# Attention tiled by 128 instead of 112 queries, the last 64 queries of two heads over one another, V loaded by batch

## The chip, the cores and the metric

The kernel runs on one core of a Trainium2 chip. A core has a matrix engine (PE, which loads weights and then streams columns through them), a vector engine (DVE), a scalar engine (ACT), a general engine (POOL), and a queue engine (SP) that issues most loads. Times are device microseconds of the whole program. The time of a kernel is the median of its runs.

## The reference

Causal attention over 4 batches, 12 heads, 448 positions and 64 dimensions a head, all in f32. The heads are then joined into rows of 768, which go through an MLP with a leaky activation.

```python
scores = scale * np.matmul(q, k.transpose(0, 1, 3, 2))   # q, k, v: (4, 12, 448, 64)
scores = np.where(mask, -1000000000.0, scores)           # mask: keys after the query
scores = scores - np.max(scores, axis=-1, keepdims=True)
attn = np.exp(scores)
attn = attn / (np.sum(attn, axis=-1, keepdims=True) + 1e-09)
attn_out = np.matmul(attn, v)
x = attn_out.transpose(0, 2, 1, 3).reshape(4 * 448, 768)
h = x @ w_in                                             # (768, 2048)
g = np.maximum(h, 0.0) + alpha * np.minimum(h, 0.0)
out = g @ w_out                                          # (2048, 768)
```

## The kernel before

The work has two parts. The first is attention, over 24 pairs of heads (`pairs`: four batches of six). The second is the MLP, whose weights arrive as 64-bit floats and are taken apart on the chip into two f32r pieces each (`decode_piece`, on DVE, POOL and ACT); its matmuls (`h_unit`, `o_tile`) begin while the last pairs of attention are still under way.

In attention the head's dimension lies on the partitions: a pair has head 0 on partitions 0 to 63 and head 1 on 64 to 127 (`half(j)`). The 448 queries are cut into four chunks of `CP` = 112. For each pair p, chunk i and head j:

- `load` (steps LQ, LK) brings Q and K, and `load_v` (LV) brings V of this pair: 112 rows of 2 KB.
- `scores` (S0, S1, S2) multiplies query chunk i with the keys up to its end. The two heads' matmuls use different rows of the array and run side by side; each head has its own PSUM bank. S0 makes chunks 1 and 0, S1 chunk 2, S2 chunk 3.
- `row_max` (MXij, DVE) adds the mask, scales, and takes the row's minimum in one pass, in place.
- `row_exp` (EXij, ACT) takes the exponential and the row's sum; `row_rec` (RC, DVE) the reciprocals of all eight sums of the pair; `row_norm` (NOij, POOL) multiplies.
- `transpose_p` (PTi, PE) transposes the probabilities in blocks of 112 by 112, 20 of them a pair; `pt_copy` (Cij, ACT or DVE) copies them out of PSUM into `ptf`, block c of chunk i at place i + 3c.
- `av` (AV) multiplies them with V, for each block c of keys all queries from there on. The two heads use different columns of the array and write the two halves of one bank.
- `x_hi` and `x_lo` (XH, XL) split the result into two f32r pieces for the MLP.

The order of all this is written out by hand in `ORDER`, which `attention` walks once per step n: an entry `NAME+lag` runs the step for pair n - lag, and a letter a, d or p says ACT, DVE or POOL. So in one step PE does AV of pair n - 4, transposes of n - 3 and scores of n - 1. Each engine works through its instructions strictly in this order and waits on semaphores. `early_steps`, `h_next` and `decode_start` are hung on entries of the last pairs. ED is one instruction of the decoding of the first weights, in each step from pair 4 on.

PSUM has eight banks, given out by `bank` in the order of their release. A pair takes 13 of them: six for scores, six for transposes, one for AV.

Of the kernel before, what the change touches and what calls it, by code (L numbers as in the profile page):

```python
# [32 lines left out]
def kernel(  # L33
# [132 lines left out]
    def load_v(p):
        b, hp = pairs[p]
        T["v", p] = ap["v"].tile([CP, NCH, 2, D], F32, tag="v", name=f"v_{p}")
        nc.sync.dma_start(out=T["v", p].rearrange("p c j d -> p (c j) d"), in_=v[b, hp])

    def copy(out, x, eng, side=1.0):
        if eng is nc.scalar:
# [4 lines left out]
            eng.tensor_scalar(out=out, in0=x, scalar1=side, scalar2=1.0, op0=ALU.mult, op1=ALU.mult)  # L177


    def scores(p, n):  # L180


        banks = [bank(f"s_{p}_{n}_{j}")[:CP] for j in range(2)]
        o = 0
        for i in ((1, 0), (2,), (3,))[n]:
            lim = (i + 1) * CP
            for j, ps in enumerate(banks):
                nc.tensor.matmul(  # L188
                    ps[:, o : o + lim], T["q", p][half(j), i * CP : (i + 1) * CP],
                    T["k", p][half(j), :lim], start=(o == 0), stop=(n > 0 or i == 0),  # L190
                )
            for j, ps in enumerate(banks):
                T["s", p, i, j] = ps[:, o : o + lim]
            o += lim

    def row_max(p, i, j):


        t = T["s", p, i, j]
        nm = T["nm", p, i, j] = ap["b4"].tile([CP, 1], F32, tag="nm", name=f"nm_{p}_{i}_{j}")  # L200
        nc.vector.tensor_tensor_reduce(  # L201
            out=t, in0=t, in1=maskb[:, (NCH - 1 - i) * CP :], scale=-SCALE, scalar=MOST_F32,
            op0=ALU.add, op1=ALU.min, accum_out=nm,
        )

    def row_exp(p, i, j):
        lim = (i + 1) * CP
        if ("p", p, i) not in T:
            T["p", p, i] = ap["p"].tile([CP, 2, lim], F32, tag=f"p{i}", name=f"p_{p}_{i}")
        if ("sm", p) not in T:  # L210
            T["sm", p] = ap["b2"].tile([CP, 2 * NCH], F32, tag="sm", name=f"sm_{p}")
        z = 2 * i + j
        nc.scalar.activation(  # L213
            T["p", p, i][:, j], T.pop(("s", p, i, j)), AF.Exp, scale=-1.0,
            bias=T.pop(("nm", p, i, j)), accum_out=T["sm", p][:, z : z + 1],
        )
# [12 lines left out]
    def transpose_p(p, i, *heads):
        t = T["p", p, i]
        for js in heads:
            ps = bank(f"pt_{p}_{i}_{js[0]}")[:CP, : len(js) * (i + 1) * CP]
            ps = T["pt", p, i, js] = ps.rearrange("p (j c n) -> p j c n", j=len(js), n=CP)
            for j in js:
                for c in range(i + 1):
                    nc.tensor.transpose(  # L238
                        ps[:, j - js[0], c], t[:, j, c * CP : (c + 1) * CP], ident[:CP, :CP]
                    )  # L240

    def pt_copy(p, i, js, eng):
        if ("ptf", p) not in T:
            T["ptf", p] = ap["pt"].tile([CP, 2, 3 * NCH + 1, CP], F32, tag="ptf", name=f"ptf_{p}")
        copy(T["ptf", p][:, js[0] : js[-1] + 1, i : 4 * i + 1 : 3], T.pop(("pt", p, i, js)), eng)

    def av(p):

        out = T["a", p] = bank(f"a_{p}")[:, :S]
        for c in range(NCH):  # L250
            for j in range(2):
                x = T["ptf", p][:, j].rearrange("p x n -> p (x n)")
                nc.tensor.matmul(  # L253
                    out[half(j), c * CP :], T["v", p][:, c, j],
                    x[:, 4 * c * CP : (3 * c + NCH) * CP], start=(c == 0), stop=(c == NCH - 1),
                )

    def x_cut(p):
# [7 lines left out]
        h, l = x_cut(p)  # L266
        nc.vector.tensor_tensor(out=l, in0=T.pop(("a", p)), in1=h, op=ALU.subtract)
# [12 lines left out]
    for i in range(NCH):  # L280
        heads = ((0, 1),) if i < 2 else ((0,), (1,))
        add(steps, f"PT{i}", transpose_p, i, *heads)
        for js in heads:
            add(choice, f"C{i}{js[0]}", pt_copy, i, js)
        for j in range(2):
# [245 lines left out]
```

## Time and profile before

| | |
|---|---|
| median of three runs | 651.55 us (650.79 to 652.76) |
| the profiled execution | 650.67 us, span 648.9 us |
| granted PE clock, mean | 0.995 |
| attention, first scores to the end of pair 23's scores | 5.1 to 164.3 us |
| overlap of attention's end with the MLP | 164.4 to 231.8 us |
| MLP alone | 231.8 to 648.9 us |

The busy share of an engine counts every moment in which one of its instructions runs. For PE that is any part of its array. "PEld" is PE's weight loading, which overlaps its matmuls. In a timeline a row begins with its start and length in us, joins equal instructions that follow each other (x16), and ends with the idle time before it and what ended that, where there was any. A group's row ends with its count, busy time and the mean of one in ns.

### The profile page before, as it was taken

The page shows a single profiled execution, that of the slowest core. Times are in us where ns is not written, and L with a number is a line of the kernel's source. Part 1 is how long each engine was busy: PE and PEld are TensorE (multiplying, and loading weights), DVE is VectorE, ACT ScalarE, POOL GpSimd, SP SyncE. Part 2 cuts the span into 40 slices and gives each one's busy share as a digit, 9 for nine tenths or more (in the row PEclk, how much of TensorE's full clock was granted, in tenths as well). Part 3 has the DMA queues.
Part 4 walks back from the last instruction along what each step waited for, and adds up shares of the span by engine and source line. Part 5 has one row for each costly group of instructions (what it writes and reads, how often), then busy time and mean ns, then how long its engine had stood idle before and what let it go on. Part 6 is the DMA issues. An engine that isn't in the chain of part 4 may idle for free.

```text
span 648.9 us, 10886 instructions
## 1 busy us (share of the span) xinstructions
PE 639.7 (99%) x3753; PEld 547.4 (84%) x3753; DVE 473.8 (73%) x1213; ACT 227.0 (35%) x662; POOL 296.6 (46%) x394
## 2 busy tenths in 40 slices
PE   7999999999999999999999999999999999999997
PEld 4667767667679989998999999899989999998997
DVE  4688787787785866887877777677877678775444
ACT  6789988889523432111111111111111111111010
POOL 3456566565555534454433434454344435443110
PEclk8999999999999999999999999999999999999999
DMA  5434434336050302032002203020330202000223
GB/s 141 135 88 111 145 98 113 99 94 200 5 195 0 97 2 97 1 98 80 19 22 78 97 1 99 27 71 1 97 98 1 78 21 98 0 2 2 97 98 146
DMA packets 32439, 47.90 MB, mean 74 GB/s; under 512 B 5248, under 2 KB 23936, under 8 KB 32384
## 3 DMA queue, kind: packets, MB, share of 16 engines
q1 hardware_dynamic: 32224, 46.98, 23.2%
q8 instruction: 30, 0.49, 0.3%
q10 hardware_dynamic: 160, 0.23, 0.1%
q14 instruction: 25, 0.20, 0.1%
HBM read 41.69 MB, written 5.51 MB: 73 GB/s over the span
## 4 chain that ended last, share of the span: by engine, by line
PE 87%; POOL 5%; issue 4%; DVE 3%; ACT 1%; POOLq 0%; DVEq 0%; ACTq 0%
PE o L352 33%; PE h L318 31%; PE a L253 8%; PE pt L238 7%; PE s L188 7%; POOL p L177 2%; ACT p L213 1%; POOL gl L338 1%; PE warm L147 1%; POOL wi L128 1%; POOL wo L128 1%; POOL y_i L124 1%; POOL y_o L124 0%; DVE g L328 0%; DVE x_i L115 0%
## 5 line engine op out<-in xcount | busy, mean ns | idle before, releaser
L352 PE MATMUL o<-wo,gh 128*128 128x384 f32 x896 | 229.3, 337 | 0.9 <-DVE g L332 0.9
L318 PE MATMUL h<-xh,wi 128*128 128x512 f32 (+1 forms) x768 | 218.2, 364 | 0.1
L338 POOL TENSOR_TENSOR gl<-g,gh 128x512 fp32r<-128x512 f32 (+1 forms) x64 | 74.2, 1159 | 254.8 <-ACT gh L337 237.6
L352 PEld LDWEIGHTS o<-wo,gh 128*128 128x128 f32 x896 | 162.3, 188 | 3.2 <-DVE g L332 1.2
L318 PEld LDWEIGHTS h<-xh,wi 128*128 128x128 f32 x768 | 138.6, 189 | 22.7 <-ACT ptf L173 0.3
L352 PE MATMUL o<-wo,gl 128*128 128x384 f32 x448 | 150.7, 336 | 0.0
L337 ACT ACTIVATE gh<-g 128x512 fp32r<-128x512 f32 (+1 forms) x64 | 37.0, 579 | 297.6 <-DVE g L332 297.6
L318 PE MATMUL h<-xl,wi 128*128 128x512 f32 (+1 forms) x384 | 139.4, 363 | 0.0
L360 DVE TENSOR_TENSOR acc<-o,acc 128x384 f32<-128x384 f32 x196 | 102.9, 553 | 42.7 <-PE o L352 41.5
L177 POOL TENSOR_SCALAR p<-p,rs 112x224 f32<-112x224 f32 (+1 forms) x192 | 92.9, 505 | 73.1 <-PE s L188 46.1
L213 ACT ACTIVATE p<-s,nm 112x224 f32<-112x224 f32 (+1 forms) x192 | 93.8, 496 | 25.9 <-DVE nm L201 25.3
L328 DVE TENSOR_SCALAR g<-h,alpha_sb 128x512 f32<-128x512 f32 (+1 forms) x64 | 43.5, 680 | 75.5 <-POOL gl L338 48.2
L201 DVE CUSTOM_DVE_ANT_0 s<-s,maskb 112x224 f32<-112x224 f32 (+1 forms) x192 | 79.9, 478 | 7.1 <-PE s L188 7.1
L352 PEld LDWEIGHTS o<-wo,gl 128*128 128x128 f32 x448 | 84.1, 188 | 0.0
L318 PEld LDWEIGHTS h<-xl,wi 128*128 128x128 f32 x384 | 72.4, 189 | 10.4
L253 PEld LDWEIGHTS a<-ptf,v 112*64 112x64 f32 x384 | 36.4, 136 | 39.2 <-issue 13.8
L253 PE MATMUL a<-ptf,v 112*64 112x448 f32 (+3 forms) x384 | 65.3, 406 | 0.1
L238 PE MATMUL pt<-ident,p 112*112 112x112 f32 x480 | 53.5, 267 | 3.6 <-POOL p L177 2.7
L238 PEld LDWEIGHTS pt<-ident,p 112*112 112x112 f32 x480 | 47.5, 136 | 8.4 <-POOL p L177 3.9
L188 PE MATMUL s<-kr,qr 64*112 64x224 f32 (+3 forms) x384 | 54.3, 414 | 0.0
L173 ACT ACTIVATE ptf<-pt 112x224 f32<-112x224 f32 (+1 forms) x96 | 41.0, 488 | 4.0 <-PE pt L238 4.0
L332 DVE SCALAR_TENSOR_TENSOR g<-h,g 128x512 f32<-128x512 f32 (+1 forms) x64 | 40.0, 625 | 2.2
(42 smaller groups left out, 528.3 us busy)
## 6 DMA issues: line engine op xcount, KB each, us to landing
wi<-in_moe_w_in_dram SPq DMA_DIRECT2D x32, 384.0 KB, 4.4
wo<-in_moe_w_out_dram SPq DMA_DIRECT2D x32, 384.0 KB, 5.5
qr<-in_q_dram SPq DMA_DIRECT2D x48, 112.0 KB, 2.7
v<-in_v_dram SPq DMA_DIRECT2D x24, 224.0 KB, 3.0
kr<-in_k_dram SPq DMA_DIRECT2D x46, 112.0 KB, 2.8
out_dram<-acc SPq DMA_DIRECT2D x13, 384.0 KB, 2.3
out_dram<-acc SPq DMA_DIRECT2D x2, 192.0 KB, 1.9
kr<-in_k_dram ACTq DMA_DIRECT2D x2, 112.0 KB, 3.6
```

Source lines behind the costliest of these rows:

```text
L173: eng.activation(out, x, AF.Copy, scale=side)
L177: eng.tensor_scalar(out=out, in0=x, scalar1=side, scalar2=1.0, op0=ALU.mult, op1=ALU.mult)
L188: nc.tensor.matmul(ps[:, o : o + lim], T["q", p][half(j), i * CP : (i + 1) * CP], T["k", p][half(j), :lim], start=(o == 0), stop=(n > 0 or ...
L201: nc.vector.tensor_tensor_reduce(out=t, in0=t, in1=maskb[:, (NCH - 1 - i) * CP :], scale=-SCALE, scalar=MOST_F32, op0=ALU.add, op1=ALU.min ...
L213: nc.scalar.activation(T["p", p, i][:, j], T.pop(("s", p, i, j)), AF.Exp, scale=-1.0, bias=T.pop(("nm", p, i, j)), accum_out=T["sm", p][:, ...
L238: nc.tensor.transpose(ps[:, j - js[0], c], t[:, j, c * CP : (c + 1) * CP], ident[:CP, :CP])
L253: nc.tensor.matmul(out[half(j), c * CP :], T["v", p][:, c, j], x[:, 4 * c * CP : (3 * c + NCH) * CP], start=(c == 0), stop=(c == NCH - 1),)
L318: nc.tensor.matmul(ps[:, :T], w[kk], x[:, kk, t0 : t0 + T], start=(n == 0), stop=(n == 3 * KD - 1),)
L328: nc.vector.tensor_scalar(out=t[:, :T], in0=ps, scalar1=0.0, scalar2=alpha_sb[:, ch : ch + 1], op0=ALU.min, op1=ALU.mult,)
L338: nc.gpsimd.tensor_tensor(out=gl[:, :T], in0=t[:, :T], in1=gh[:, :T], op=ALU.subtract)
L352: nc.tensor.matmul(ps[:, :NH], x[:, t * P : (t + 1) * P], w, start=(n == 0), stop=(n == 3 * GC - 1),)
L360: nc.vector.tensor_tensor(out=a[:, cols], in0=ps[:, :NH], in1=a[:, cols], op=ALU.add)
```

## The change

Queries are cut into three chunks of 128 (`QP`) and one of 64. The last chunk of both heads is put into one tile: head 0 on partitions 0 to 63, head 1 on 64 to 127. So S2 writes one bank instead of two, one mask pass, one exponential and one scaling serve both heads (MX30, EX30, NO30), and four transposes of 128 by 128 instead of eight of 112 by 112 move them. One copy, C30, takes both heads into `ptf`; C31 no longer exists. Keys are cut in blocks of 128, the last of them with 64 rows and 64 rows of zeros, so AV contracts over 128 rows and its matmuls have 448, 320, 192 and 64 columns instead of 448, 336, 224 and 112. A pair has 7 mask passes, exponentials and scalings instead of 8, 16 transposes instead of 20, and 11 PSUM banks instead of 13.

V is still stored in chunks of 112 rows, so it is loaded for a whole batch of six pairs into one of two buffers, in seven loads that regroup the rows into blocks of 128, in pieces of 512 bytes. The first batch is loaded whole in step 1, later ones over four steps, one batch ahead. The order is another one: XH goes from ACT to DVE, C00 from ACT to DVE, and K is loaded a step earlier, just ahead of Q.

```diff
 CP = 112
+QP = 128
 ORDER = """
-NO11+3p LK+1 MX11+2 EX10+2 EX20+2 AV+4 MX00+2 EX11+2 EX00+2 PT0+3 PT1+3 LV+3 MX21+2 PT2+3 EX21+2 MX31+2 NO31+3p MX30+2 MX01+2 EX31+2 EX01+2 XH+4a NO30+3p PT3+3 C00+3a XL+4 C10+3a C20+3a S0+1 S1+1 ED+1 EX30+2 C21+3d LQ+0 RC+2 MX10+1 NO10+2p S2+1 NO21+2p NO01+2p C30+3a NO00+2p NO20+2p MX20+1 C31+3d
+NO00+3p NO10+3p MX11+2 NO21+3p NO11+3p EX10+2 EX11+2 MX20+2 NO20+3p MX21+2 EX20+2 NO30+3p MX00+2 EX00+2 AV+4 LV+4 PT1+3 PT0+3 PT2+3 EX21+2 MX01+2 EX01+2 C10+3a MX30+2 XH+4d ED+1 XL+4 EX30+2 C00+3d C21+3d RC+2 NO01+2p C20+3a LK+0 LQ+0 PT3+3 S0+1 S1+1 C30+3a MX10+1 S2+1
 """
...
+def load_v(b):
+    for n in range(NQ + 1):
+        o, end = 0, min(QP, S - n * QP)
+        while o < end:
+            c, x = divmod(n * QP + o, CP)
+            w = min(end - o, CP - x)
+            nc.sync.dma_start(
+                out=vs[b % 2][o : o + w, :, n].rearrange("r h j d -> r h (j d)"),
+                in_=v[b, :, x : x + w, 2 * c : 2 * c + 2].rearrange("h r j d -> r h (j d)"),
+            )
+            o += w
+            yield
...
+def load_v_next(p):
+    if p < 4 or (p >= NPAIR - 1 and (p + 1) % NPAIR < 4):
+        load_v_some(2 if p < 3 or (p + 1) % NPAIR < 3 else 1)
...
 def scores(p, n):
+    if n == 2:
+        ps = bank(f"s_{p}_{n}")[:, :S]
+        for j in range(2):
+            nc.tensor.matmul(
+                ps[half(j)], T["q", p][half(j), NQ * QP :], T["k", p][half(j)],
+                start=True, stop=True,
+            )
+        T["s", p, NQ, 0] = ps
+        return
...
 def transpose_p(p, i):
+    for js in ((0,), (1,)) if i == 2 else (range(t.shape[1]),):
...
+            for c in range(i + 1):
+                nc.tensor.transpose(ps[:, j - js[0], c], t[:, j, c * QP : (c + 1) * QP], ident)
...
 def pt_copy(p, i, j, eng):
+    if i < NQ:
+        copy(out[:, j : j + t.shape[1]], t, eng)
+    else:
+        copy(out[:, :, :, :LQ], t[:, 0].rearrange("p c (j n) -> p j c n", j=2), eng)
...
 def av(p):
+    for c in range(NQ + 1):
         for j in range(2):
+            x = T["ptf", p][:, j].rearrange("p x n -> p (x n)")[:, 3 * c * QP :]
             nc.tensor.matmul(
+                out[half(j), c * QP :], vs[b % 2][:, hp, c, j], x[:, c * QP : S],
+                start=(c == 0), stop=(c == NQ),
             )
...
+masks.extend(ap["p3"].tile([P, w], BF16, name=f"mask{w}") for w in (NQ * QP, S))
+v_loads = (x for b in range(B) for x in load_v(b))
+after(1, "LQ", load_v_some, 7)
-after(last - 1, "C31", h_finish)
+after(last - 1, "C30", h_finish)
```

Three places show how the rows move. The first is PE in the middle of attention, from the last score block of one pair (`s_2`) over AV (`a`) and the transposes (`pt`) of earlier pairs. Before:

```order
L188 MATMUL s_2_0_935<-kr_841,qr_819 112x448
L188 MATMUL s_2_1_936<-kr_841,qr_819 112x448
L253 MATMUL a_958<-ptf_908,v_873 64x448 x2
L253 MATMUL a_958<-ptf_908,v_873 64x336 x2
L253 MATMUL a_958<-ptf_908,v_873 64x224 x2
L253 MATMUL a_958<-ptf_908,v_873 64x112 x2
L238 MATMUL pt_0_0_972<-ident,p_0_863 112x112 x2
L238 MATMUL pt_1_0_975<-ident,p_1_846 112x112 x4
L238 MATMUL pt_2_0_984<-ident,p_2_849 112x112 x3
L238 MATMUL pt_2_1_988<-ident,p_2_849 112x112 x3
L238 MATMUL pt_3_0_1005<-ident,p_3_893 112x112 x4
L238 MATMUL pt_3_1_1010<-ident,p_3_893 112x112 x4
```

After the change the same place reads:

```order
L217 MATMUL s_2_776<-kr_659,qr_662 64x448 x2
L298 MATMUL a_801<-ptf_737,v_136 64x448 x2
L298 MATMUL a_801<-ptf_737,v_136 64x320 x2
L298 MATMUL a_801<-ptf_737,v_136 64x192 x2
L298 MATMUL a_801<-ptf_737,v_136 64x64 x2
L279 MATMUL pt_1_0_812<-ident,p_1_692 128x128 x4
L279 MATMUL pt_0_0_817<-ident,p_0_706 128x128 x2
L279 MATMUL pt_2_0_820<-ident,p_2_701 128x128 x3
L279 MATMUL pt_2_1_824<-ident,p_2_701 128x128 x3
L279 MATMUL pt_3_0_853<-ident,p_138 128x128 x4
```

The order of the three blocks stays; the last score block now writes one bank, chunk 1 is transposed ahead of chunk 0, and chunk 3 needs four transposes for both heads.

The second place is DVE, from XL (`xl`) of one pair to the masks of a later one (rows `ISA`, the second of each two reads out the minimum `nm`). `x_i` is the decoding step, `sm` and `rs` are RC. Before:

```order
L267 TENSOR_TENSOR xl<-a_529,xh 128x448
L114 TENSOR_SCALAR x_i_0_492<-x_i_0_492 128x384
L175 COPY ptf_587<-pt_2_1_560 112x3x112
L221 TENSOR_TENSOR sm_525<-sm_525,least 112x8
L222 RECIPROCAL rs_608<-sm_525 112x8
L201 ISA s_0_0_592,nm_1_0_611<-s_0_0_592,maskb 112x224
L201 ISA nm_1_0_611 112x1
L201 ISA s_1_0_598,nm_2_0_623<-s_1_0_598,maskb 112x336
L201 ISA nm_2_0_623 112x1
L175 COPY ptf_587<-pt_3_1_582 112x4x112
```

After the change:

```order
L203 CAST xh<-a_518 128x448
L115 TENSOR_SCALAR x_i_0_457<-x_i_0_457 128x384
L312 TENSOR_TENSOR xl<-a_518,xh 128x448
L203 COPY ptf_549<-pt_0_0_534 128x2x128
L203 COPY ptf_549<-pt_2_1_541 128x3x128
L263 TENSOR_TENSOR sm_503<-sm_503,least 128x7
L264 RECIPROCAL rs_559<-sm_503 128x7
L240 ISA s_0_0_575,nm_1_0_586<-s_0_0_575,mask_113 128x256
```

XH and C00 came to DVE, C31 (`pt_3_1`) behind the second mask is gone.

The third place is SP at the start, from the loads of pair 1. Before:

```order
L160 DMA kr_147<-in_k_dram 64x448 x2
L160 DMA qr_185<-in_q_dram 64x448 x2
L160 DMA kr_205<-in_k_dram 64x448 x2
L169 DMA v_228<-in_v_dram 112x512
L160 DMA qr_278<-in_q_dram 64x448 x2
```

After the change:

```order
L161 DMA qr_147<-in_q_dram 64x448 x2
L182 DMA v_136<-in_v_dram 112x6x128
L182 DMA v_136<-in_v_dram 16x6x128
L182 DMA v_136<-in_v_dram 96x6x128
L182 DMA v_136<-in_v_dram 32x6x128
L182 DMA v_136<-in_v_dram 80x6x128
L182 DMA v_136<-in_v_dram 48x6x128
L182 DMA v_136<-in_v_dram 64x6x128
L161 DMA kr_199<-in_k_dram 64x448 x2
L161 DMA qr_202<-in_q_dram 64x448 x2
```

The seven loads of V's first batch now stand between the loads of pairs 1 and 2.

More of the change, by code (lines that the diff above doesn't have):

```diff
@@ L73 @@
     ident = const.tile([P, P], F32, name="ident")
-    least = const.tile([CP, 2 * NCH], F32, name="least")
-    maskb = const.tile([CP, S], BF16, name="maskb")
+    least = const.tile([P, 2 * NQ + 1], F32, name="least")
     alpha_sb = const.tile([P, DFF // P], F32, name="alpha_sb")
@@ L147, in warm @@
             nc.tensor.matmul(ps, warm_sb[:, :P], warm_sb, start=True, stop=True)
-    T = {}
+    T, vs, p3, masks = {}, [], [], []
     def half(j):
@@ L164, in load_first, with open_v, load_v_some @@
         load(0, "k", nc.scalar)
[L166 to L169, printed above, removed]
+    def open_v():
+        for n in range(2):
+            vs.append(ap[f"v{n}"].tile([P, NPAIR, NQ + 1, 2, D], F32, name=f"v{n}"))
+            nc.gpsimd.memset(vs[n][LQ:, :, NQ], 0.0)
+            p3.append(ap["p3"].tile([P, (NQ + 1) * QP], F32, name=f"p3{n}"))
+            nc.gpsimd.memset(p3[n][:, S:], 0.0)
+    def load_v(b):
[10 more added lines that the diff above has]
+                yield
+    def load_v_some(n):
+        for _ in range(n):
+            next(v_loads, 0)
+    def load_v_next(p):
+        if p < 4 or (p >= NPAIR - 1 and (p + 1) % NPAIR < 4):
+            load_v_some(2 if p < 3 or (p + 1) % NPAIR < 3 else 1)
     def copy(out, x, eng, side=1.0):
@@ L177, in copy @@
             eng.tensor_scalar(out=out, in0=x, scalar1=side, scalar2=1.0, op0=ALU.mult, op1=ALU.mult)
+    heads = [((0,), (1,))] * NQ + [((0, 1),)]
     def scores(p, n):
-        banks = [bank(f"s_{p}_{n}_{j}")[:CP] for j in range(2)]
+        if n == 2:
[7 more added lines that the diff above has]
+            return
+        banks = [bank(f"s_{p}_{n}_{j}") for j in range(2)]
         o = 0
-        for i in ((1, 0), (2,), (3,))[n]:
-            lim = (i + 1) * CP
+        for i in ((1, 0), (2,))[n]:
+            lim = (i + 1) * QP
             for j, ps in enumerate(banks):
                 nc.tensor.matmul(
-                    ps[:, o : o + lim], T["q", p][half(j), i * CP : (i + 1) * CP],
+                    ps[:, o : o + lim], T["q", p][half(j), i * QP : (i + 1) * QP],
                     T["k", p][half(j), :lim], start=(o == 0), stop=(n > 0 or i == 0),
                 )
-            for j, ps in enumerate(banks):
                 T["s", p, i, j] = ps[:, o : o + lim]
@@ L199, in row_max @@
         t = T["s", p, i, j]
[L200 removed]
+        nm = T["nm", p, i, j] = ap["b4"].tile([P, 1], F32, tag="nm", name=f"nm_{p}_{i}_{j}")
         nc.vector.tensor_tensor_reduce(
[L202 to L203 removed]
+            out=t, in0=t, in1=masks[1] if i == NQ else masks[0][:, (NQ - 1 - i) * QP :],
+            scale=-SCALE, scalar=MOST_F32, op0=ALU.add, op1=ALU.min, accum_out=nm,
         )
     def row_exp(p, i, j):
[L207 removed]
         if ("p", p, i) not in T:
[L209 removed]
+            if i == NQ:
+                T["p", p, i] = p3[p % 2].unsqueeze(1)
+            else:
+                T["p", p, i] = ap["p"].tile([P, 2, (i + 1) * QP], F32, tag=f"p{i}", name=f"p_{p}_{i}")
         if ("sm", p) not in T:
[L211 removed]
+            T["sm", p] = ap["b2"].tile([P, 2 * NQ + 1], F32, tag="sm", name=f"sm_{p}")
         z = 2 * i + j
+        t = T.pop(("s", p, i, j))
         nc.scalar.activation(
[L214 removed]
+            T["p", p, i][:, j, : t.shape[1]], t, AF.Exp, scale=-1.0,
             bias=T.pop(("nm", p, i, j)), accum_out=T["sm", p][:, z : z + 1],
@@ L277 @@
         steps["L" + nm.upper()] = lambda p, nm=nm: p and load(p, nm)
-    for n in range(NCH - 1):
+    for n in range(NQ):
         add(steps, f"S{n}", scores, n)
[L280 to L285, printed above, removed]
+    for i in range(NQ + 1):
+        add(steps, f"PT{i}", transpose_p, i)
+        for j in range(2 if i == 2 else 1):
+            add(choice, f"C{i}{j}", pt_copy, i, j)
+        for j in range(2 if i < NQ else 1):
             add(steps, f"MX{i}{j}", row_max, i, j)
@@ L431 @@
         make_identity(nc, ident)
-        nc.gpsimd.memset(maskb, 0.0)
+        open_pools(att_b, "left", {"v1": 1, "p3": 1, "pt": 2, "b2": 2, "b4": 8, "p": 2})
+        masks.extend(ap["p3"].tile([P, w], BF16, name=f"mask{w}") for w in (NQ * QP, S))
+        for t in masks:
+            nc.gpsimd.memset(t, 0.0)
         nc.gpsimd.memset(least, 1e-9)
-        mk = ap["mk"].tile([CP, CP], F32, name="mk")
+        mk = ap["mk"].tile([P, QP], F32, name="mk")
         nc.gpsimd.memset(mk, 0.0)
         nc.gpsimd.affine_select(
-            out=mk, in_=mk, pattern=[[-1, CP]], compare_op=ALU.is_ge, fill=NEG, base=0,
+            out=mk, in_=mk, pattern=[[-1, QP]], compare_op=ALU.is_ge, fill=NEG, base=0,
             channel_multiplier=1,
         )
-        nc.scalar.activation(maskb[:, S - CP :], mk, AF.Copy)
+        nc.scalar.activation(masks[0][:, (NQ - 1) * QP :], mk, AF.Copy)
+        for j in range(2):
+            rows = slice(j * LQ, (j + 1) * LQ)
+            nc.scalar.activation(masks[1][rows, NQ * QP :], mk[rows, rows], AF.Copy)
         warm(WARM)
-        open_pools(att_b, "left", {"v": 3, "pt": 2, "b2": 2, "b4": 8, "p": 2})
+        open_v()
         early = early_chunk()
@@ L456 @@
         after(last - 1, "PT3", h_next)
-        after(last - 1, "C31", h_finish)
-        after(last - 1, "C31", decode_start, 2)
+        after(last - 1, "C30", h_finish)
+        after(last - 1, "C30", decode_start, 2)
         after(last - 1, "AV", h_next)
@@ L461 @@
         after(last, "C21", h_finish)
-        after(last, "C31", decode_finish, 2)
-        after(last, "C31", decode_start, 3)
+        after(last, "C30", decode_finish, 2)
+        after(last, "C30", decode_start, 3)
         after(last, "AV", h_next)
```

34 lines of the change are left out of this document (15 added, 19 removed).

## The prediction

> **What bounds the kernel now.** I read the busy shares of the page first, then the chain of waits in order of time, then the timeline of one pair, and last the groups by shape.
>
> ```profile
> PE 639.7 (99%) x3753; PEld 547.4 (84%) x3753; DVE 473.8 (73%) x1213; ACT 227.0 (35%) x662; POOL 296.6 (46%) x394
> ```
>
> TensorE (PE) is busy for 99% of the span. That alone says little, since a PE that runs half of its array also counts as busy. The chain of waits (start, length, what) shows the rhythm of the attention part:
>
> ```profile
> 91.55 2.06 PE pt L238 x20
> 93.60 2.08 PE s L188 x16
> 95.68 2.66 PE a L253 x14
> 98.35 2.06 PE pt L238 x20
> ```
>
> One pair takes 2.06 (transposes) + 2.08 (scores) + 2.66 (AV) = 6.80 us, and every piece of it is PE. The timeline of that pair (start, length, engine, what, idle before it) shows what hides in the 2.66:
>
> ```profile
> 92.79 0.62 DVE L267 TENSOR_TENSOR xl<-a,xh 128x448 fp32r<-128x448 f32 x1 [0.95 <-ACT xh L173]
> 93.33 0.55 DVE L119 SCALAR_TENSOR_TENSOR y_i<-wi,x_i 128x384 int32<-128x384 int32 x1
> 93.80 0.50 DVE L175 COPY ptf<-pt 112x336 f32<-112x336 f32 x1
> ...
> 94.43 0.17 DVE L221 TENSOR_TENSOR sm<-sm,least 112x8 f32<-112x8 f32 x1
> ...
> 94.82 0.37 DVE L201 CUSTOM_DVE_ANT_0 s<-s,maskb 112x224 f32<-112x224 f32 x1
> 95.07 3.81 POOL L177 TENSOR_SCALAR p<-p,rs 112x224 f32<-112x224 f32 x8 [2.99 <-PE s L188]
> ...
> 95.57 0.62 DVE L175 COPY ptf<-pt 112x448 f32<-112x448 f32 x1
> ...
> 95.61 2.73 PE L253 MATMUL a<-ptf,v 112*64 112x448 f32 x16
> ...
> 96.11 0.39 DVE L201 CUSTOM_DVE_ANT_0 s<-s,maskb 112x224 f32<-112x224 f32 x1
> ...
> 96.25 1.89 PEld L253 LDWEIGHTS a<-ptf,v 112*64 112x64 f32 x14 [0.44 <-DVE ptf L175]
> ...
> 96.42 0.32 DVE L201 CUSTOM_DVE_ANT_0 s<-s,maskb 112x112 f32<-112x112 f32 x1
> ...
> 96.65 0.55 DVE L201 CUSTOM_DVE_ANT_0 s<-s,maskb 112x336 f32<-112x336 f32 x1
> ...
> 97.11 0.67 DVE L201 CUSTOM_DVE_ANT_0 s<-s,maskb 112x448 f32<-112x448 f32 x1
> ...
> 97.70 0.67 DVE L201 CUSTOM_DVE_ANT_0 s<-s,maskb 112x448 f32<-112x448 f32 x1
> ...
> 98.28 0.76 PEld L238 LDWEIGHTS pt<-ident,p 112*112 112x112 f32 x8
> ```
>
> AV starts at 95.61 with head 0. Head 1, which uses the other 64 columns of the array, gets its weights only at 96.25, when the vector engine (DVE) has ended the copy C31 that began at 95.57. For about 0.6 us half the array waits. Near the end of attention one AV runs without that wait, from its start to that of the MLP matmul behind it:
>
> ```profile
> 175.48 2.11 PE L253 MATMUL a<-ptf,v 112*64 112x448 f32 x16
> 177.52 0.50 PE L318 MATMUL h<-xh,wi 128*128 128x512 f32 x1
> ```
>
> It takes 2.04 us, so the wait costs 2.66 - 2.04 = 0.62 us a pair. How many pairs run in this rhythm is read from the PE's timeline: scores of pair 2 start in the first row, those of pair 23 in the second, 21 pairs and 144.7 us apart (6.89 each; a few pairs are some tenths longer than 6.80).
>
> ```profile
> 17.34 2.87 PE L188 MATMUL s<-kr,qr 64*112 64x224 f32 x16
> 162.08 2.33 PE L188 MATMUL s<-kr,qr 64*112 64x224 f32 x16
> ```
>
> **PE, block by block.** Two shapes of one group give the price of a column:
>
> ```profile
> L188 PE MATMUL s<-kr,qr 64*112 64x448 f32 x96 | 23.6, 541 | 0.0
> L188 PE MATMUL s<-kr,qr 64*112 64x112 f32 x96 | 9.6, 263 | 0.0
> ```
>
> (541 - 263) / 336 = 0.83 ns a column and pass; each f32 matmul has two passes (16 records for 8 matmuls). The heads run side by side, so scores and AV stream 1120 columns twice, 2240, and the 20 transposes of 112 columns 2240 as well: 1.86 us each. What is left, 0.22 of 2.08, 0.18 of 2.04, 0.20 of 2.06, is the price of changing the shape of the array three times a pair.
>
> - Scores: 256 + 128 + 384 + 448 = 1216 columns a head instead of 1120, so 2432 x 0.83 = 2.02, plus 0.22. The last chunk has both heads over one another (64 rows by 64 columns each), which is one more change of shape. No row shows its cost: 0 if it hides as between blocks of one shape, 0.22 if it is like the three others. I take 0.12, nearer to the middle. Scores: 2.36 (2.24 to 2.46). A loss of 0.28.
> - Transposes: 16 of 128 columns instead of 20 of 112: 2048 x 0.83 + 0.20 = 1.90, a gain of 0.16. What may spoil it is the weight load, longer for 128 columns:
>
> ```profile
> L318 PEld LDWEIGHTS h<-xh,wi 128*128 128x128 f32 x768 | 138.6, 189 | 22.7 <-ACT ptf L173 0.3
> L238 PEld LDWEIGHTS pt<-ident,p 112*112 112x112 f32 x480 | 47.5, 136 | 8.4 <-POOL p L177 3.9
> ```
>
>   If a transpose grew as these loads do, 16 x 2.06/20 x 189/136 = 2.29. A load overlaps the matmul ahead, so I take 1.90 and keep 2.29 for the range.
> - AV: 448 + 320 + 192 + 64 = 1024 columns instead of 1120: 2048 x 0.83 + 0.18 = 1.88. C31 is gone; one copy C30 on the scalar engine (ACT) brings the last chunk for both heads, so the 0.62 goes if that copy is in time: 2.66 - 1.88 = 0.78 gained.
>
> A pair: 2.36 + 1.90 + 1.88 = 6.14 us (6.02 at the cheapest, 6.63 at the dearest), 0.66 under 6.80, if nothing else becomes late.
>
> **What could be late instead.** DVE: from start to start, the mask-and-minimum takes 0.23 for 112 columns (96.42 to 96.65), 0.31 for 224, 0.46 for 336, 0.59 for 448. Between these lie 0.24, 0.35 and 0.51 for 128, 256, 384. Before: 2 x (0.23 + 0.31 + 0.46 + 0.59) = 3.18; after, with one pass of 448 for both heads: 2 x (0.24 + 0.35 + 0.51) + 0.59 = 2.79. Taken away: C31, 0.54 (95.57 to 96.11). Added: XH, a 448-column copy like it, 0.54, and C00 of 256 columns, about 0.34; C21 grows from 336 to 384 columns, 0.42 to 0.47 (a record of 0.50, less the same 0.08 by which 0.54 is under 0.62). XL 0.54, one decoding step 0.47, sums and reciprocal 0.39 stay. Total 5.54 of 6.14, against 5.54 of 6.80 before. DVE gets no lighter, and its slack shrinks from 1.26 to 0.60. The wait of XL on ACT's XH (0.95) disappears, as both now stand on one engine, but XH itself waits for the end of AV, with everything behind it (XL, C00, C21, sums, first mask). I follow one pair with time 0 at the start of AV: AV ends at 1.88, XH starts at about 2.1, the rest takes 0.54 + 0.47 + 0.54 + 0.34 + 0.47 + 0.39 and ends at 4.85. The first score block (384 columns twice, 0.64, and 0.2) ends at 1.88 + 1.90 + 0.84 = 4.62. The masks then run to 4.85 + 2.79 = 7.64, that is 1.50 in the next pair, ahead of its AV's end. So it closes, with 0.6 us to spare.
>
> ACT has the most to spare afterwards. Its rows:
>
> ```profile
> 92.22 0.53 ACT L173 ACTIVATE xh<-a 128x448 fp32r<-128x448 f32 x1
> 92.65 1.13 ACT L173 ACTIVATE ptf<-pt 112x224 f32<-112x224 f32 x3
> ...
> 97.09 0.34 ACT L213 ACTIVATE p<-s,nm 112x112 f32<-112x112 f32 x1
> ...
> 97.42 0.54 ACT L213 ACTIVATE p<-s,nm 112x336 f32<-112x336 f32 x1
> ...
> 97.93 0.64 ACT L213 ACTIVATE p<-s,nm 112x448 f32<-112x448 f32 x1
> ```
>
> It loses XH (0.43 from start to start), one copy of 224, and one exponential in eight. C10, EX30, C20, C30 follow the transposes: with copies at 1.13 for 1008 columns about 0.57 + 0.64 + 0.43 + 0.57 = 2.2 after PT1's end, while the next AV starts 12 transposes and the scores later, 12 x 0.106 + 2.36 = 3.6. So C30 is 1.4 us early, and the cover of AV's last input is thicker than now. POOL scales 1984 columns a pair instead of 2240 and idles 2.99 of each pair before; the five results that PT1 waits for need some 2.3 us, and RC to the next PT1 are over 4 us. PSUM blocks a pair fall from 13 to 11 for the same 8 banks; those that scores reuse are freed by C10, EX30, XL and C20, each 0.6 us or more ahead in the walk above.
>
> SP (the load queue) issues seven loads of V for the first batch ahead of K and Q of pair 2:
>
> ```profile
> 10.18 0.59 SPq L169 DMA_DIRECT2D v<-in_v_dram  x1
> q1 hardware_dynamic: 32224, 46.98, 23.2%
> ```
>
> Seven issues are 7 x 0.59 = 4.1 us, from about 4.5 to 8.6, and K and Q behind them are out at about 11. A batch is 2688 pieces of 512 bytes. The mean piece of the queue cost 0.232 x 648.9 x 16 / 32224 = 75 ns of one of 16 engines and had 1458 bytes, so a batch needs at most 12.6 us, and by bytes 4.4. It lands between 11 and 18; the scores that need pair 2 began at 17.34, the first AV at 20.13. I take nothing, and up to 1 us for the range. Later batches have four pairs' time to land in the other buffer.
>
> **Start and end.** In the start (PE's timeline) the first transposes wait for POOL:
>
> ```profile
> 13.23 4.18 PE L238 MATMUL pt<-ident,p 112*112 112x112 f32 x20 [2.30 <-POOL p L177]
> ```
>
> They end when scaling ends. Masks are 0.4 shorter (2.79 for 3.18), scaling about 0.4 (1984 columns for 2240 at 3.81), with fewer transposes behind: 1.0 us gained, between -1 (late V) and 2.5. At the end of attention the MLP's first matmuls fill the PE:
>
> ```profile
> 164.40:231.80 67.40, 65.09 (x371) 55.69 (x370) 51.28 (x104) 23.64 (x59) 37.09 (x42) 1.00 0.21 71
> 168.96 0.59 PE L238 MATMUL pt<-ident,p 112*112 112x112 f32 x4 [0.37 <-POOL p L177]
> 170.49 0.59 PE L238 MATMUL pt<-ident,p 112*112 112x112 f32 x4 [0.93 <-ACT p L213]
> ```
>
> Three AVs and two blocks of transposes get 0.16 shorter each, 0.8 together, and one AV still has its 0.6 wait; 0.37 + 0.93 of stalls may move. But the decoding of weights on DVE and POOL may hold the end: 0 to 3, I take 1.2. The MLP behind it is the same code and I cost it at nothing.
>
> **Sum.** 21 x 0.66 = 13.9, + 1.0 + 1.2 = 16.1. The profiled execution took 650.67 (span 648.9), so 634.6; the median of the runs shown is 0.9 higher, 651.55, and I forecast 635.
>
> **Rivals.**
> 1. DVE becomes the bound. For it: 5.54 busy in 6.14, and an in-order queue that waits for PE twice in each pair. If half of its present idle time of 1.26 stays, a pair takes 6.17, if three quarters stay 6.48. Against it: most of that idle time was the wait on XH. At 6.48: 650.67 - 21 x 0.32 - 1.0 = 643.
> 2. The last score chunk does not run side by side. Its two heads sit in different rows of the array but write one PSUM bank, while in every score matmul of before the heads write two banks. If they took turns, four passes of 448 would follow each other: 4 x 448 x 0.83 = 1.49 instead of 0.74, a pair 6.88, and the time 650.67 + 21 x 0.08 - 2.2 = 650.2, no change. The Trainium skill ("TensorEngine Tiling (Array Packing)", Restrictions and Gotchas, PSUM Pressure) says that different row tiles cannot access the same PSUM bank simultaneously. No score row of before has two row tiles in one bank, so the trace cannot decide it. Against the rival: AV of before has two heads in one bank, in two halves of its partitions as here, and runs at the full column rate (2.04).
> 3. Slower: the same place, but each turn also empties the array, 0.2 us as at the changes of shape. Four turns add 0.8, a pair is 7.68, and the time 650.67 + 21 x 0.88 - 2.2 = 667. It decides from the point where this chunk costs 1.6 us: a pair of 7.0, 2 us over before.
>
> **Chances.** Forecast 0.78. DVE as bound 0.14: slack is thin. Turns in one bank without emptying 0.04, with it 0.04, as AV's rows speak against both. About 0.3% (2 us) can be told from no change here: rivals 1 and the forecast are faster (0.92), rival 2 the same, rival 3 slower. Low end: a pair at 6.02 gives 21 x 0.78 = 16.4, with 2.5 and 3 at the ends 628.8. High end: 643 takes in rival 1 and a pair of 6.5 with dear transposes, and leaves out about 0.1 above.
>
> **What would show it.** In the chain: transposes 1.9, scores 2.3 to 2.4, AV 1.9, a pair of 6.1. In the waits: no AV waiting for DVE's ptf. XH among DVE's rows, started by the end of AV. If scores take 3.1 or more, rival 2 or 3 holds; if PE's transposes or scores wait for DVE and a pair is 6.4, rival 1. Wrong too if AV stays at 2.5 with a wait for ACT's C30, or the first AV comes after 21 us behind V's loads.

## The result: 632.6 us, and the profile after

The changed kernel takes 632.60 us (median of four runs, 632.30 to 633.05), against 651.68 us (650.79 to 652.76) for the kernel before in the same session. The ratio is 0.9707 (95% interval 0.969 to 0.9724). The profiled span went from 648.9 to 630.8 us.

First the chain of waits of the changed kernel for two pairs (start, length, what):

```profile
88.77 1.90 PE pt L279 x16
90.67 1.50 PE s L228 x12
92.17 0.90 PE s L217 x4
93.06 1.88 PE a L298 x16
94.95 1.90 PE pt L279 x16
96.84 1.50 PE s L228 x12
```

A pair takes 6.18 us (90.67 to 96.84), and all of it is PE: transposes 1.90, scores 1.50 + 0.90 = 2.40, AV 1.88. Before, it was 2.06, 2.08 and 2.66. So all work on PE together costs the same as before without AV's wait (2.06 + 2.08 + 2.04 = 6.18 also): the dearer scores (+0.32) eat up what transposes and AV save (0.16 each). The gain in the steady rhythm is the wait that is gone.

The timeline of the changed kernel shows what became of the disputed places:

```profile
92.10 0.97 PE L217 MATMUL s<-kr,qr 64*64 64x448 f32 x4
...
94.99 0.62 DVE L203 CAST xh<-a 128x448 fp32r<-128x448 f32 x1 [0.46 <-PE a L298]
...
96.73 0.98 ACT L201 ACTIVATE ptf<-pt 128x384 f32<-128x384 f32 x2
```

The last score block takes four passes (two heads, two passes each) in 0.97, so the heads run side by side in their one bank; taking turns would have needed 1.49 by the prediction's estimate. XH on DVE now waits 0.46 for the end of AV: that is what DVE has to spare in this pair (over all pairs 5.2 us in 13 waits between 60 and 140 us, 0.40 each). ACT's copies of the last chunks (C20, then C30) begin at 96.73 and last 0.98, while the next AV starts at 99.24 (93.06 + 6.18).

PE's timeline at the start:

```profile
12.31 0.44 PE L279 MATMUL pt<-ident,p 128*128 128x128 f32 x2 [2.07 <-POOL p L205]
13.33 1.87 PE L279 MATMUL pt<-ident,p 128*128 128x128 f32 x14 [0.58 <-POOL p L205]
16.02 2.02 PE L228 MATMUL s<-kr,qr 64*128 64x256 f32 x12 [0.81 <-DMA qr<-in_q_dram]
```

The seven loads of V ahead of Q cost a wait of 0.81 there. Scores of pair 2 start at 16.02, before at 17.34. Most of this difference is not the change's doing. A row of windows gives the stretch in us, its length, the busy time of PE, PEld, DVE, ACT and POOL, the granted clock, the DMA share and GB/s. Around the first transposes it reads, before:

```profile
13.20:17.34 4.14, 4.11 (x21) 3.52 (x21) 2.29 (x10) 4.04 (x15) 2.16 (x5) 0.50 0.47 133
```

and after:

```profile
12.30:16.00 3.70, 2.31 (x16) 1.71 (x17) 2.82 (x12) 3.62 (x14) 2.15 (x4) 1.00 1.11 237
```

In the profiled execution of the kernel before, the first 20 transposes ran at half the clock and took 4.18 us; those of later pairs take 2.06. The profiled execution of the changed kernel was spared this. Experiments 7, 11 and 12 come back to it.

And the last pair of attention:

```profile
146.19 1.57 PE L228 MATMUL s<-kr,qr 64*128 64x256 f32 x12
```

From pair 2 to pair 23 it is 130.17 us now and was 144.74: 14.57 less. The period explains 21 x 0.62 = 13.0 of it. Most of the rest is that four pairs of before were clearly longer than 6.80: the first two, with 7.34 and 7.22, and two in the middle with 7.21 each. After the change only the first is longer, by 0.4. The timeline of before shows one of the two in the middle:

```profile
79.62 0.55 ACT L127 ACTIVATE wi<-y_i 128x384 fp32r<-128x384 f32 x1
80.04 0.66 ACT L213 ACTIVATE p<-s,nm 112x448 f32<-112x448 f32 x1
...
80.82 0.17 DVE L221 TENSOR_TENSOR sm<-sm,least 112x8 f32<-112x8 f32 x1 [0.74 <-ACT p L213]
...
82.64 1.89 PEld L253 LDWEIGHTS a<-ptf,v 112*64 112x64 f32 x14 [0.68 <-DVE ptf L175]
```

Where the decoding of weights puts its copy (L127) into ACT's queue, the exponential behind it comes later, the sums (L221) on DVE wait 0.74 for it, and with them all that stands behind them, C31 too. The second head of AV then waits 0.68 for C31 instead of 0.44. In the chain of waits this pair's scores take 2.26 instead of 2.08 and its AV 2.89 instead of 2.66. After the change the same copies stand in ACT's queue (the first at 71.41), and no pair is longer than 6.18 for it.

### The profile page after: what moved, and what is told of

It reads as the page before. It is cut to its first block, busy times and chain, and to the rows that moved or that the text cites. A ratio compares the mean times of both kernels' runs of the same rounds, so it can differ in the third digit from the quotient of the medians.

```text
span 630.8 us, 10560 instructions
## 1 busy us (share of the span) xinstructions
PE 619.7 (98%) x3657; PEld 525.1 (83%) x3657; DVE 476.5 (76%) x1189; ACT 203.3 (32%) x568; POOL 289.3 (46%) x375
## 4 chain that ended last, share of the span: by engine, by line
PE 92%; DVE 2%; DMA 2%; POOL 2%; issue 1%; SPq 1%; ACT 0%; POOLq 0%
PE h L362 35%; PE o L396 34%; PE pt L279 7%; PE a L298 7%; PE s L228 5%; PE s L217 3%; DMA qr<-in_q_dram 1%; DMA v<-in_v_dram 1%; SPq L161 1%; POOL p L205 1%; POOL y_i L125 0%; POOL gl L382 0%; DVE g L372 0%; DVE x_i L116 0%; DVE x_i L115 0%
## 5 line engine op out<-in xcount | busy, mean ns | idle before, releaser
L205 POOL TENSOR_SCALAR p<-p,rs 128x128 f32<-128x128 f32 (+3 forms) x168 | 82.7, 513 | 64.0 <-DVE rs L264 41.1
L255 ACT ACTIVATE p<-s,nm 128x256 f32<-128x256 f32 (+3 forms) x168 | 81.6, 493 | 18.5 <-DVE nm L240 18.2
L240 DVE CUSTOM_DVE_ANT_0 s<-s,mask 128x256 f32<-128x256 f32 (+3 forms) x168 | 70.1, 489 | 7.5 <-PE s L228 6.7
L298 PEld LDWEIGHTS a<-ptf,v 128*64 128x64 f32 x384 | 25.4, 136 | 34.3 <-ACT p L255 15.5
L279 PE MATMUL pt<-ident,p 128*128 128x128 f32 x384 | 47.8, 276 | 3.7 <-POOL p L205 3.7
L279 PEld LDWEIGHTS pt<-ident,p 128*128 128x128 f32 x384 | 41.5, 141 | 6.9 <-POOL p L205 5.0
L298 PE MATMUL a<-ptf,v 128*64 128x448 f32 (+3 forms) x384 | 46.8, 386 | 0.0
L201 ACT ACTIVATE ptf<-pt 128x512 f32<-128x512 f32 (+1 forms) x72 | 37.8, 564 | 16.4 <-PE pt L279 16.4
L228 PE MATMUL s<-kr,qr 64*128 64x384 f32 (+2 forms) x288 | 38.4, 394 | 0.8 <-DMA qr<-in_q_dram 0.8
```

The lines of the kernel that those rows point to most:

```text
L228: nc.tensor.matmul(ps[:, o : o + lim], T["q", p][half(j), i * QP : (i + 1) * QP], T["k", p][half(j), :lim], start=(o == 0), stop=(n > 0 or ...
L240: nc.vector.tensor_tensor_reduce(out=t, in0=t, in1=masks[1] if i == NQ else masks[0][:, (NQ - 1 - i) * QP :], scale=-SCALE, scalar=MOST_F3 ...
L255: nc.scalar.activation(T["p", p, i][:, j, : t.shape[1]], t, AF.Exp, scale=-1.0, bias=T.pop(("nm", p, i, j)), accum_out=T["sm", p][:, z : z ...
L279: nc.tensor.transpose(ps[:, j - js[0], c], t[:, j, c * QP : (c + 1) * QP], ident)
L298: nc.tensor.matmul(out[half(j), c * QP :], vs[b % 2][:, hp, c, j], x[:, c * QP : S], start=(c == 0), stop=(c == NQ),)
```

## The experiments

The comparison with the kernel before is given each time as ratio and 95% interval. Entries of `ORDER` are written one to a line.

**1. C31 earlier.** In the kernel before, DVE makes C31 before the sums and the first mask instead of behind the second mask.

```diff
 C21+3d
+C31+3d
 LQ+0
...
 MX20+1
-C31+3d
```

> The kernel before, with one entry of its order moved: the copy C31 stands ahead of RC on DVE instead of behind the second mask of the next pair. Theory W (the pair of 6.80 us is PE's 6.18 plus the wait of AV for C31, nothing else): the wait goes, a pair takes about 6.2, the time is about 638. Theory L (the pair of 6.80 is a loop through DVE and ACT: first mask 0.54, eight exponentials 3.76, XH 0.53, XL 0.54, decoding step 0.47, C21 0.42, RC 0.39, together 6.65, and AV's wait only fills what PE has left): C31 now lies inside the loop, which becomes about 7.2, and the time is about 659.

Measured: 648.66 us (648.37 to 649.56), 0.9965 (0.9952 to 0.9978). AV did lose its wait, but something else got it. The chain of waits of this kernel:

```profile
91.33 2.04 PE a L253 x16
93.37 1.03 PE pt L238 x9
```

AV takes 2.04. The transposes now wait for POOL instead, as PE's row shows:

```profile
94.92 0.50 PE L238 MATMUL pt<-ident,p 112*112 112x112 f32 x3 [0.25 <-POOL p L177]
```

In the list of waits "PEld pt L238 <- POOL p L177" sums up to 6.5 us in 18 waits between 40 and 160 us. The sums, and with them the scaling, now stand behind C31 (0.54) in DVE's queue. A pair takes about 6.55. Over 21 pairs that is 7 us less than the 6.89 of before, but the stretch behind pair 23's scores is 4.8 us longer (491.6 for 486.8). There the edit moves more than the copy: decoding steps of later weights (`decode_start`) are hung on C31 and come along with it. In the chain of waits they now stand on DVE ahead of the sums of the last pair:

```profile
169.58 0.62 DVE x_o L113 x2
...
175.56 0.09 DVE sm L221
```

In the kernel before they start at 176.98, behind these sums (172.54). So the time of this run is not that of the copy alone; the 6.55 of a pair is. Neither theory held as written: the wait moved, and kept more than half of its length.

**2. XH to DVE.** In the kernel before, `XH+4a` becomes `XH+4d`.

```diff
-XH+4a
+XH+4d
```

> The kernel before, with XH on DVE instead of ACT, C31 where it was. Theory W: no change, since C31 is where it was: 651. Theory L: XL no longer waits for the exponentials on ACT, the loop falls to about 6.0 to 6.3 and what is left of AV's wait sets a pair of 6.3 to 6.5: 639 to 645.

Measured: 647.48 us (646.62 to 647.59), 0.994 (0.9922 to 0.9959). A pair takes 6.63, with AV at 2.49, still waiting for C31. A small gain, between the two theories.

**3. Both at once.** XH to DVE and C31 to ACT, tiling by 112 as before.

```diff
-XH+4a
+XH+4d
...
 C30+3a
+C31+3a
...
-C31+3d
```

> The kernel before, with XH on DVE and C31 on ACT just behind C30; tiling by 112, eight masks and exponentials as before. Theory W: about 638, as in the first. Theory L: the loop is cut and C31 early, a pair of 6.2 to 6.3, 637 to 640. If instead the work on ACT (about 5.9 us a pair, with a decoding copy of 0.55 in some) needs the new tiling, a pair stays over 6.5: over 644.

Measured: 636.35 us (636.04 to 636.72), 0.9773 (0.9758 to 0.9788). The chain of waits:

```profile
92.12 2.08 PE s L188 x16
94.20 2.04 PE a L253 x16
96.23 2.06 PE pt L238 x20
```

The same 6.18 a pair as the changed kernel, without a change of tiling. Two entries of the order bring about three quarters of the gain (2.27% of 2.93%). What the changed kernel has beyond this (3.75 us) lies at the ends: pair 2 starts 1.8 earlier, and the stretch behind pair 23's scores is 2.0 shorter. Not all of that is the tiling's. In the profiled execution of this run the first 20 transposes took 3.83 us, at a granted clock of 0.56, which the changed kernel was spared; and about 1.5 is the layout of memory (experiments 5 and 6).

**4. The changed kernel with XH back on ACT.**

```diff
-XH+4d
+XH+4a
```

> The changed kernel, with XH back on ACT. Theory W: nothing waits for it in PE, no change, 632.6. Theory L: the loop first mask 0.55, six exponentials 2.72, C10 0.57, XH 0.53, XL 0.54, decoding step 0.47, C00 0.34, C21 0.47, RC 0.39 is 6.6 us, over PE's 6.18, and the time about 641.

Measured: 634.97 us (634.53 to 635.14), 0.9751 (0.9736 to 0.9765). XL waits for XH (in the list of waits "DVE xl L312 <- ACT xh L201: 28.7, 22, 2.4", so 1.3 a pair), and still most pairs take 6.18 to 6.22; one takes 6.31, three take about 6.5, and the first is longer. With XH away, DVE has room for most of that wait. The move is worth 2.4 us in this kernel. In experiment 2 XH was on DVE and a pair took 6.63, with C31 behind the masks; so it seems that the loss of C31 mattered more, which no run tests in the changed kernel by itself.

**5 and 6. The layout of on-chip memory.** The MLP is the same code, but its stretch was shorter after the change. The groups of its output matmuls, before:

```profile
L352 PE MATMUL o<-wo,gh 128*128 128x384 f32 x896 | 229.3, 337 | 0.9 <-DVE g L332 0.9
L352 PE MATMUL o<-wo,gl 128*128 128x384 f32 x448 | 150.7, 336 | 0.0
```

and after:

```profile
L396 PE MATMUL o<-wo,gh 128*128 128x384 f32 x896 | 228.0, 335 | 1.3 <-DVE g L376 1.3
L396 PE MATMUL o<-wo,gl 128*128 128x384 f32 x448 | 150.0, 335 | 0.0
```

The same 1344 matmuls take 380.0 us before and 378.0 after. In the chain of waits a block of 48 of them takes 8.44 or 8.46 in 11 of 20 cases before, and 8.32 to 8.35 everywhere after. The half of the streamed weights `wo` that is allotted last lies 896 bytes lower after the change, since the masks (448 values of 2 bytes) moved to another pool. 896 is three and a half times 256. Theory A: the place decides, and repeats every 256 bytes, so that 128 bytes more turn the one case into the other. So an unused tile of 128 bytes is put ahead, once into the kernel of experiment 3 and once into the changed kernel.

```diff
+    pad = const.tile([P, 32], F32, name="pad")
```

> The kernel before with XH on DVE and C31 on ACT (which took 636.35), and an unused tile of 128 bytes a partition among the constants, so that everything behind it in the core's memory lies 128 bytes further. Theory A (address: in the MLP, the output blocks of every second group take 8.46 us before and 8.34 after the change, since the new kernel's constants are 896 bytes smaller and shift the weights' tiles): all output blocks take 8.34, the MLP is 1.6 to 2 us shorter, 634.5. Rival B (the slower blocks come from something else in the tiling, such as the loads): no change, 636.3.

> The changed kernel with the same unused tile of 128 bytes. Theory A: the output blocks of every second group rise from 8.34 to 8.46 us and the time to about 634.3. Rival B: no change, 632.6.

Measured: experiment 3 with the tile 634.82 us (634.58 to 637.13), 0.9763 (0.9742 to 0.9784); the changed kernel with the tile 634.39 us (633.86 to 634.93), 0.9749 (0.9734 to 0.9763). One is 1.5 faster for it, the other 1.8 slower. A block in the chain of waits of the first:

```profile
371.87 8.34 PE o L353 x48
```

and of the second:

```profile
370.27 8.46 PE o L397 x48
```

The two swapped their block times, as theory A says. Part of the gain of the change is an accident of where the weights lie. That 256 is the period is a guess: four layouts fit it, and no more were tried.

**7. V's first loads split.** Four of them stand behind pair 1's Q as before, three behind pair 2's Q.

```diff
-        after(1, "LQ", load_v_some, 7)
+        after(1, "LQ", load_v_some, 4)
+        after(2, "LQ", load_v_some, 3)
```

> The changed kernel with the seven loads of the first batch of V split: four behind Q of pair 1, three behind Q of pair 2. In the changed kernel PE stands idle 0.81 us at 16.02 for Q of pair 2, behind V's loads. If the loads' place is the cause, that wait goes, scores of pair 2 start at about 15.2, and the time falls by about 0.8 to 631.8, unless the first AV then waits for V. If the load engines are simply full until then (0.88 of their time over the first 16 us), the wait moves to V and the time stays 632.6.

Measured: 633.02 us (630.99 to 633.31), 0.9721 (0.9702 to 0.974). No gain, though the wait for Q is gone. PE's timeline, and the window of the same stretch:

```profile
13.69 2.92 PE L279 MATMUL pt<-ident,p 128*128 128x128 f32 x14 [0.58 <-POOL p L205]
16.54 2.16 PE L228 MATMUL s<-kr,qr 64*128 64x256 f32 x12
```

```profile
13.69:16.54 2.85, 2.85 (x14) 2.37 (x15) 1.57 (x6) 2.50 (x10) 1.13 (x2) 0.62 1.02 220
```

The 14 transposes took 2.92 instead of 1.87 at a granted clock of 0.62. One of the four runs was at 630.99, with a mean granted clock of 1.000, the others at 632.9 to 633.3, with 0.997. Experiments 11 and 12 ask whether the idle time of 2.1 us ahead of these transposes brings this on.

**8. Masks and exponentials of the last chunk apart.** The changed kernel, with the two heads' last score chunk in two banks, each with its own mask pass and exponential on its 64 partitions (the scaling, transposes and C30 stay joined).

```diff
-            ps = bank(f"s_{p}_{n}")[:, :S]
             for j in range(2):
+                ps = bank(f"s_{p}_{n}_{j}")[half(j), :S]
...
 MX30+2
+MX31+2
...
 EX30+2
+EX31+2
```

> The changed kernel with the last chunk's scores in two banks, and masks and exponentials of the two heads apart (8 each a pair instead of 7); scaling, transposes and copies stay joined. DVE gets 0.59 us more a pair, ACT 0.61. If PE's 6.18 us bounds and DVE has 0.6 to spare, a pair takes 6.2 to 6.3 and the time is 633 to 636. If the joined mask and exponential are what brought the gain, a pair takes 6.7 to 6.8 and the time is 643 to 646. The last score block takes 0.90 us in one bank; if one bank made the heads take turns in any part, two banks would be shorter.

Measured: 645.05 us (644.76 to 646.41), 0.9919 (0.99 to 0.9937). Most of the gain is gone. The group of the last score block reads the same in both kernels,

```profile
L217 PE MATMUL s<-kr,qr 64*64 64x448 f32 x96 | 23.3, 562 | 0.0
```

so two heads in one bank cost nothing. But a pair took 6.59 in the mean, the scores waiting for PSUM banks (2.85 for 2.40). Was DVE the bound, or the third bank?

**9. The same with XH on ACT,** to take 0.54 off DVE.

> The kernel with the masks and exponentials of the last chunk apart for the two heads and its scores in two banks, with XH moved from DVE to ACT in addition (0.54 less on DVE of a pair, one wait of XL for ACT more). Theory: DVE was the bound there, in need of 6.59 us a pair with the decoding step. Then its need falls to about 6.05, the pair comes down to 6.2 to 6.4 and the time to 636 to 641. Rival: the third PSUM bank of the scores is what delays them, or XL's wait for ACT eats the gain; then the pair stays at 6.5 to 6.6 and the time at 643.5 to 646.

Measured: 647.72 us (645.77 to 648.71), 0.994 (0.9921 to 0.9959); 6.71 a pair. Neither theory as written. DVE had room now (busy 80.85 of 90 us from 60 to 150, against 86.33 in experiment 8), but ACT's queue held XH ahead of two exponentials (EX30, EX31), and the second head's first score matmul waited for a bank that they free. This run could not tell the bank from the work.

**10. The same with the scores in one bank,** and XH on DVE again: the second mask and the second exponential are then all that is left of experiment 8.

```diff
+            both = bank(f"s_{p}_{n}")[:, :S]
             for j in range(2):
-                ps = bank(f"s_{p}_{n}_{j}")[half(j), :S]
+                ps = both[half(j)]
```

> The kernel with masks and exponentials of the last chunk apart for the two heads, but its scores in one bank again, so that a pair takes 11 PSUM banks as in the changed kernel and not 12. In the kernels with 12 banks the second head's first score matmul waits 0.4 us for a bank that an exponential (EX30) or XL sets free. If that bank is the loss, the pair comes back to 6.18 to 6.25 and the time to 633 to 636. If the work of the second mask pass and the second exponential on DVE and ACT is the loss, the pair stays at 6.4 to 6.6 and the time at 641 to 646. In between, both have a part.

Measured: 645.76 us (645.75 to 646.28), 0.9916 (0.9898 to 0.9934); 6.61 a pair. The bank is not the loss, the work is. The chain of waits runs through DVE alone (from the two mask passes of the last chunk on):

```profile
101.91 0.52 DVE s L243
...
102.52 0.64 DVE s L243
...
103.29 0.62 DVE xh L203
...
103.95 0.56 DVE x_i L124
104.51 0.54 DVE xl L321
105.04 0.80 DVE ptf L203 x2
105.84 0.08 DVE sm L272
```

Pairs take 6.53 or 6.74. With the joined pass DVE has 0.40 to spare in 6.18; a second pass asks for 0.61 of its own (101.91 to 102.52), and DVE becomes the bound. That makes 6.18 - 0.40 + 0.61 = 6.39; the other 0.2 of the 6.61 lies between XH and the next first mask (2.96 for 2.74 in the changed kernel), in gaps of some hundredths whose cause was not followed. So the joined mask pass is the part of the tiling without which this order would not hold 6.18.

**11 and 12. Idle matmuls at the start.** Eight of the matmuls with which the program begins (`warm`) are put behind the last scores of pair 1, where PE waits for POOL: once in the changed kernel, once in that of experiment 7.

```diff
+        after(1, "S2", warm, 8)
```

> The changed kernel with eight idle matmuls (the ones that the program begins with) behind the last scores of pair 1, in the 2.07 us in which PE waits for POOL at the start. Nothing else is moved, and the wait for Q of pair 2 (0.81) stays. If the idle stretch is what brings the phase of half clock in some runs (3.4 us long, 1 to 1.3 us lost), the runs lie at 631.6 to 632.6 and the profiled run has no half clock behind 12 us. If the idle matmuls come in the way of the first transposes, or the half clock has another cause, 632.6 to 633.5.

> The changed kernel with V's first loads split over two steps, as before, and the eight idle matmuls behind the last scores of pair 1. If the half clock behind the idle stretch ate the 0.8 us that the split gave, the runs lie together at 631.0 to 631.8 and no half clock shows in the profiled run after 12 us. If the half clock has another cause, they are split again between 631.0 and 633.1.

Measured: the changed kernel with them 632.17 us (631.93 to 632.38), 0.9705 (0.9691 to 0.9719); with V split as well 631.51 us (631.30 to 631.97), 0.9695 (0.9681 to 0.9709). PE's timeline of the second:

```profile
11.08 1.90 PE L148 MATMUL warm<-warm_sb 128*128 128x512 bf16 x8
13.05 0.44 PE L279 MATMUL pt<-ident,p 128*128 128x128 f32 x2
14.06 1.88 PE L279 MATMUL pt<-ident,p 128*128 128x128 f32 x14 [0.58 <-POOL p L205]
15.87 1.57 PE L228 MATMUL s<-kr,qr 64*128 64x256 f32 x12
```

The transposes are back at 1.88. In all ten runs of the two versions the mean granted clock was 0.999 or 1.000; without the idle matmuls it was 0.997 in five of the eight runs of the changed kernel and of experiment 7. That fits the idle stretch as what brings the low clock on. With V split as well all five runs lie together, below every run of the changed kernel (632.30 and more), though the intervals of the two ratios overlap. By the medians this version beats both, the changed kernel by 1.1 us. Alone, either edit moves the median by 0.4 us or less.

## Why the prediction was right, point by point

The forecast was 635 us in a range of 629 to 643, and faster; 632.6 came. In spans the gain was 18.1 us against a sum of 16.1:

| term | predicted | measured |
|---|---|---|
| 21 pairs | 13.9 | 14.57 |
| start (scores of pair 2: 17.34, now 16.02) | 1.0 | 1.32 |
| end of attention, to the end of the second stretch of `o_tile` | 1.2 | 1.44 |
| the MLP behind it | 0 | 0.78 |

- **PE's blocks** were right: scores 2.36 predicted and 2.40 measured, transposes 1.90 and 1.90, AV 1.88 and 1.88. The extra change of shape, taken at 0.12, is the term that was small by 0.04.
- **AV's wait** went, and C30 came in time, as the prediction said. It did not say that the wait, together with C31's place, was nearly all of the gain. The prediction counted 0.62 of 0.66 a pair for it and so had the size, but it credited the change as a whole; experiment 3 shows that two entries of the order give the same period.
- **The long pairs** were mentioned ("a few pairs are some tenths longer") and left out of the sum. Four of them, 0.41 to 0.54 over 6.80, are 1.8 us, more than the 21 x 0.04 by which a pair came out longer than predicted.
- **DVE** was the thinnest step. The slack of 0.60 was mis-sized: it measures 0.40. The missing 0.2 lies in the masks, which with the last one's read-out take 2.98 (91.55 to 94.53 in the timeline of the changed kernel) instead of the 2.79 of the sum. Rival 1 did not come, but experiments 8 and 10 show how near it was: one more pass of 64 partitions turns a pair into 6.6 and the time into 645, near the 643 that the rival gave.
- **Turns in one bank** (rivals 2 and 3) did not happen. The Trainium skill ("TensorEngine Tiling (Array Packing)", Restrictions and Gotchas, PSUM Pressure) says that different row tiles cannot access the same PSUM bank simultaneously; this case does not agree for two tiles that also differ in columns and write different partitions: 0.97 for four passes of 448 columns, and the same 562 ns a matmul in one bank as in two.
- **V's loads** were taken at nothing, up to 1 us: 0.81 of waiting for Q, inside the bound.
- **The start** came near by luck. Scaling does end 0.9 earlier, at 14.45 (11.09 + 3.36) instead of 15.35 (11.54 + 3.81), close to the 0.8 that the prediction gave for masks and scaling. But the 20 transposes of before did not "end when scaling ends": they went on to 17.34, two us later, because the granted clock was 0.50. After the change the wait for Q took most of the 0.9. An estimate: at full clock the eight transposes behind the last scaling of before take 0.82 (8 of 20 in 2.06) and end at about 16.2, so that some 1.1 of the measured 1.32 is what the low clock had cost before.
- **The end** came out near. PE reaches the second stretch of `o_tile` 59.2 us after the start of pair 23's scores (205.40 - 146.19) instead of 61.3 (223.38 - 162.08), and gives 0.64 back in it. PE's timeline of the changed kernel shows two waits for DVE there, where before had one of 0.93:

```profile
212.23 0.62 PE L396 MATMUL o<-wo,gh 128*128 128x384 f32 x2 [0.42 <-DVE g L376]
...
214.47 0.62 PE L396 MATMUL o<-wo,gh 128*128 128x384 f32 x2 [0.90 <-DVE g L376]
```

- **The MLP at nothing** was the step that failed, if only by 0.8. The prediction put it at nothing because the code is the same; the place of the weights was what it left out. The 11 dear blocks fell by 0.12 each, 1.3 us, and the last 72 matmuls by 0.18. Against that, what follows the last matmuls, with the final stores, takes 0.7 longer than before (4.0 for 3.3), in every run with the new tiling, and why is open.

## What to carry to other kernels

Before a retiling is credited, the order alone should be tried: here a wait of 0.62 in nearly every pair was set by where one copy stood in an in-order queue, and two entries removed it without any new tile. A wait that is only moved along its own queue comes back elsewhere (experiment 1); it goes when the work goes to an engine that has room, or when two passes on half the partitions become one. A kernel whose edits change allotted sizes should be compared with a padded twin when 0.3% matter. And a stretch at the start is compared with the granted clock beside it: half of it can pass for a wait.

## What was not expected of the hardware

- The time of a matmul depended on where its operands lie in on-chip memory: 8.46 against 8.34 us for the same 48 matmuls, switched in both directions by 128 unused bytes. Which property of the address does it, four layouts do not settle.
- Around a stretch of 2.1 to 2.3 us without matmuls at the start, the granted clock fell to half for some microseconds in some executions (0.50 over 13.20 to 17.34 us in the kernel before; 0.62 in the mean over 13.69 to 16.54 us in experiment 7; not in the profiled execution of the changed kernel, with 2.07 us of idle time). With idle matmuls in the gap it was 1.00 in both kernels.
